# One mixture-of-experts tail: PSUM banks of its own for the fourth expert's result, ScalarE as the reader of all results but the last, and 4096 instead of 3584 columns of late weights in flight

## The chip, the cores and the metric

The kernel runs on one core of one Trainium2 chip. The metric is the device time of one execution in microseconds. The core has a matrix engine (TensorE, PE in the profile, with its weight loads shown apart as PEld), VectorE (DVE), ScalarE (ACT), GpSimd (POOL) and SyncE (SP), which issues most DMAs. Each engine does its own instructions strictly in the order written and waits for others through semaphores. TensorE writes to PSUM, eight banks of 2 KB for each of 128 partitions; VectorE and ScalarE read it from there. TensorE's clock is granted at 2.4 GHz (shown as 1.00) or 1.2 GHz (0.50).

## The reference

Attention with a soft cap, then a mixture of eight experts in which each token goes to one expert and each expert keeps at most 80 tokens:

```
scores = cap * tanh((q @ k.T) / sqrt(64) / cap);  attn = softmax(scores) @ v      # 8 x 12 heads, 448 x 64
x = attn as 3584 tokens x 768
logits = x @ w_gate                                # 768 x 8
expert = argmax(logits); gate = softmax(logits) at expert
for each expert with tokens: keep the 80 of largest gate
    out[kept] = gate[kept] * (relu(x[kept] @ w1[e]) @ w2[e])    # 768 x 1024, 1024 x 768
out of all other tokens = 0
```

## The kernel before

Attention is done for 48 pairs of heads in turn, TensorE and ScalarE being busy together. The gating logic (which tokens, in which order of gate) runs beside it on VectorE, GpSimd and ScalarE. After the last pair the tail begins: six experts that can have tokens, numbered 0 to 5 in the code (first to sixth in the text). The tokens of experts 0 to 3 are chosen from the first five batches and then corrected; those of experts 4 and 5 are known only after all rankings, so that their tokens are gathered (`xgv`, GpSimd, line 730) and transposed on VectorE (`lay`, line 1439, tile `xt`) in the middle of the tail.

The list `jobs` (line 743) fixes TensorE's order: first product of expert 0, then for each expert the first product of the next and the second of this one, as a0 a1 b0 a2 b1 a3 b2 b3 a4 a5 b4 b5. A first product has six chunks (`chunk`, line 782, tile `hp`, 32 matmuls of 80 columns each), a second product eight (`tokens`, line 792, tile `yt`, 18 matmuls of 192 or 384 columns). Between the chunks stand small products of the ranking: `pd` (line 433) counts, from 0/1 strips `gb` that VectorE makes (line 421), how many tokens come before each.

A first product goes to one of two pairs of banks (`pss`, tag `sc`) that are used in turn; `relu` (line 810, ScalarE) reads it. A second product goes to the two banks `yt0` and `yt1` of the pool `pf`, which all experts but the last share (line 1483), so that each must wait until the result before it has been read; the last uses two banks of the pool `ps1`. In a result, 80 tokens lie on partitions 0 to 79; the last quarter of the 768 columns lies on partitions 96 to 127 of both banks, in three pieces.

`weighed` (line 850) reads a result, weighs it by the gate `gt` and scatters it to HBM: VectorE copies the three pieces into the last quarter of the output tile `ywv` (line 855), ScalarE weighs the other three quarters while reading them (lines 856 and 857), VectorE weighs the last quarter in place (line 858), and GpSimd issues the scatter (line 859). There is one buffer of `ywv`. A result is read two chunks into the second product or the first product that follows it (`turns`, line 1489): the program's order on VectorE, ScalarE and GpSimd is that in which `background` (line 1283) and these calls emit their instructions.

The weights come in 84 loads of 128 rows, 1024 columns for a first product's chunk and 768 for a second's, in the order of `jobs`, through a ring of 22 buffers. `more` (line 753) adds to each load a wait for an earlier one, so that the loads from that one on have at most `FLIGHT` columns together: 5120 for the first 40 loads (`FULL`), 3584 after.

Of the kernel before, what the change touches and what calls it, by code (L numbers as in the profile page):

```python
# [7 lines left out]
F32 = mybir.dt.float32  # L8
# [3 lines left out]
AF = mybir.ActivationFunctionType  # L12
ALU = mybir.AluOpType
# [19 lines left out]
MV = 80  # L33
NV = 6
NPRE = 4
# [17 lines left out]
ODD = 'q0 q1 y b u a02 b q2 q3 x b a12 l n b'  # L53
NEXT = 'q0 q1 y b u a02 b q2 q3 x a12 l n b'
LAST = 'y q0 a00 a01 a10 a11 b a02 a12 u l n b m'
FLIGHT = (5120, 3584)
FULL = 40
PLACES = 4
GROUP = 835
# [63 lines left out]
def attn_moe(ctx, tc, q2, k, v, cap, wg, w1, w2, capacity, ct, out):  # L123
    nc = tc.nc
# [59 lines left out]
    si0 = consts.tile([SL, NPRE], I32, name="si0")  # L184
    sg0 = consts.tile([SL, NPRE], I32, name="sg0")
    gt0 = consts.tile([SL, NPRE], F32, name="gt0")
# [566 lines left out]
    def more(n):  # L753

        while len(wts) < min(n, len(jobs)):
            k_, v, kk = jobs[len(wts)]
            if v not in regs:
                src = ev0_i if v < NPRE else ev_i
                regs[v] = nc.values_load(src[0:1, v:v + 1], engines=[mybir.EngineType.SP], min_val=0, max_val=E - 1)
            wts.extend(wload(wring, regs[v], f"{v}", [kk if k_ == "a" else KD + kk], issued))  # L760
            i = len(issued) - 1
            room = FLIGHT[i >= FULL]
            while i >= 0 and room >= cols[i]:
                room -= cols[i]
                i -= 1
            if i >= 0:
                tc.add_manual_dep(issued[-1].ins, issued[i].ins.name, flight, reason="flight")
# [14 lines left out]
    def chunk(ps, x, w, kk, last, n, m=SL):  # L782

        per = n // 256
        ps = ps if isinstance(ps, list) else [ps[:, 0], ps[:, 1]]
        for j in range(n // 128):
            for h in range(2):
                nc.tensor.matmul(ps[j // per][64 * h:64 * h + 64, j % per * m:(j % per + 1) * m],  # L788
                                 w[:, 128 * j + 64 * h:128 * j + 64 * h + 64], x[:, kk, 0:m],
                                 start=(kk == 0 and j % per == 0), stop=(kk == last and j % per == per - 1))  # L790

    def tokens(ps, x, w, kk, last):


        q = DM // 4
        for r in range(2):
            for g in range(3):
                m = min(32, MV - 32 * g)
                y = slice(0, 2 * q) if r == 0 else slice(2 * q, 3 * q)
                nc.tensor.matmul(ps[r][32 * g:32 * g + m, 0:(2 - r) * q], x[:, kk, 32 * g:32 * g + m], w[:, y], start=kk == 0, stop=kk == last)  # L800
            for g in range(2 * r, 2 + r):
                m = min(32, MV - 32 * g)
                nc.tensor.matmul(ps[r][96:96 + m, g % 2 * q:g % 2 * q + q], x[:, kk, 32 * g:32 * g + m], w[:, 3 * q:4 * q],  # L803
                                 start=kk == 0 and g != 1, stop=kk == last and g > 0)
# [5 lines left out]
    def relu(fp, hp, tag, m=SL):  # L810
        th = fp.tile([128, KF, m], F32, name=f"th{tag}", tag="th")
        nc.scalar.activation(th.rearrange("p (a b) c -> p a (b c)", a=2), hp[:, :, 0:4 * m], AF.Relu)
        return th
# [33 lines left out]
                                     in_=ys.rearrange("p a b -> p (a b)"), in_offset=None,  # L847
                                     bounds_check=T - 1, oob_is_err=False)

    def weighed(fp, yt, gt, si, tag):  # L850
        q = DM // 4
        ys = fp.tile([MV, 4, q], F32, name=f"yw{tag}", tag="ys", bufs=1)
        for g in range(3):
            m = min(32, MV - 32 * g)
            nc.vector.tensor_copy(ys[32 * g:32 * g + m, 3], yt[g // 2][96:96 + m, g % 2 * q:g % 2 * q + q])
        nc.scalar.activation(ys[:, 0:2].rearrange("p a b -> p (a b)"), yt[0][0:MV, 0:2 * q], AF.Copy, scale=gt)  # L856
        nc.scalar.activation(ys[:, 2], yt[1][0:MV, 0:q], AF.Copy, scale=gt)  # L857
        nc.vector.tensor_scalar(ys[:, 3], ys[:, 3], gt, None, op0=ALU.mult)
        nc.gpsimd.indirect_dma_start(out=out, out_offset=bass.IndirectOffsetOnAxis(ap=si, axis=0),  # L859
                                     in_=ys.rearrange("p a b -> p (a b)"), in_offset=None,  # L860
                                     bounds_check=T - 1, oob_is_err=False)
# [170 lines left out]
    pss = at.enter_context(tc.tile_pool(name="pss", bufs=2, space=PSUM, side="right"))  # L1032
# [371 lines left out]
    fp = ft.enter_context(tc.tile_pool(name="fp", bufs=2, reuse_waits="tile"))  # L1404
# [6 lines left out]
    xv, fin = {}, {}  # L1411
# [47 lines left out]
    yt = {}  # L1459

    def out_(v):
        early_ = v < NPRE
        if v >= NV - 2:
            nc.gpsimd.drain()
        weighed(fp, yt[v], (gt0[:, v:v + 1] if early_ else fin["gt", v])[0:MV], (si0 if early_ else fin["si"])[0:MV, v:v + 1], f"v{v}")
    more(ahead(st["begun"]))
    turns = []
    for i, (k_, vi, kk) in list(enumerate(jobs))[st["begun"]:]:
        more(ahead(i))
        soon = jobs[min(i + 3, len(jobs) - 1)]  # L1470
        if soon[0] == "a" and soon[2] == 0 and soon[1] < NPRE - 1:
            st["there"](soon[1])
        if k_ == "a":
            if kk == 0:
                st["there"](vi)
                hp[vi] = pss.tile([128, 2, 512], F32, name=f"hp{vi}", tag="sc")
            chunk(hp[vi], xv[vi] if vi >= NPRE else xt0[vi], wts[i], kk, KD - 1, F, MV)
            if kk == KD - 1:
                ht[vi] = relu(fp, hp[vi], f"v{vi}", MV)
        else:  # L1480
            if kk == 0:
                if vi < NV - 1:
                    yt[vi] = [pf.tile([128, 512], F32, name=f"yt{vi}{i}", tag=f"yt{i}") for i in range(2)]
                else:
                    yt[vi] = [ps1.tile([128, 512], F32, name=f"yt{vi}{i}", tag="misc", bufs=2) for i in range(2)]
            tokens(yt[vi], ht[vi], wts[i], kk, KF - 1)
            if kk == KF - 1:
                turns.append(vi)
        if turns and (kk == 2 or i == len(jobs) - 1):
            out_(turns.pop())  # L1490
        background(4000, (1340, 1010)[k_ == "b"], TAIL)
# [52 lines left out]
```

## Time and profile before

| what | value |
|---|---|
| median of three runs (lowest to highest) | 486.61 us (485.44 to 486.83) |
| the profiled execution | 487.65 us, span 485.9 us |
| TensorE busy | 461.6 us, 95% of the span |
| ScalarE, GpSimd, VectorE busy | 340.1, 278.6, 278.0 us |
| granted clock of TensorE, mean | 0.986 |
| HBM traffic over the span | 202 GB/s |

The span is the time from the first to the last instruction of the profiled execution; the execution's time has 1.8 us more around it. Times in rows are microseconds from the span's start. A busy TensorE says little about where time is lost, since its matmuls are pipelined; what counts is where the rows of the tail show it idle or at the lower clock, and which engine ended the idle time.

### The profile page before, as it was taken

What the parts mean: (1) busy time and instruction counts of PE and PEld (TensorE: products, weight loads), DVE (VectorE), ACT (ScalarE), POOL (GpSimd) and SP (SyncE); (2) the same over time, 40 slices, a digit from 0 to 9 for tenths busy, and PEclk for the clock granted to TensorE, in tenths of its full rate; (3) what the DMA queues carried; (4) which work ended last, traced back from release to release, by engine and by line L of the source; (5) the groups of instructions that cost most, each with busy time, mean ns of one, the idle gap of its engine ahead of it and who ended that gap; (6) DMA issues with size and microseconds to landing.
All of it is one profiled execution on the core that took longest, in us unless ns stands there. A gap on an engine that the chain in (4) does not pass through costs nothing.

```text
span 485.9 us, 14488 instructions
## 1 busy us (share of the span) xinstructions
PE 461.6 (95%) x5864; PEld 197.2 (41%) x5864; DVE 278.0 (57%) x796; ACT 340.1 (70%) x360; POOL 278.6 (57%) x296
## 2 busy tenths in 40 slices
PE   6899999999999999999999999999999999969892
PEld 1222232223333223323233333324336887947882
DVE  1045446755664777579658957895668644633011
ACT  4999979988988998798888878886973444400010
POOL 1577686667667665776667585586496168060000
PEclk9899999999999999999999999999999999988998
DMA  5557478757836876764568377468269999999971
GB/s 150 149 163 206 110 182 240 213 139 189 228 94 168 234 189 172 185 185 133 138 169 225 100 195 209 111 190 240 71 161 387 386 349 336 336 327 306 293 267 32
DMA packets 68204, 99.09 MB, mean 204 GB/s; under 512 B 19328, under 2 KB 53152, under 8 KB 68128
## 3 DMA queue, kind: packets, MB, share of 16 engines
q1 hardware_dynamic: 63360, 83.82, 57.3%
q0 software_dynamic: 4640, 14.26, 11.3%
q8 instruction: 48, 0.79, 0.7%
q14 instruction: 28, 0.23, 0.2%
q10 hardware_dynamic: 128, 0.00, 0.0%
HBM read 74.54 MB, written 23.51 MB: 202 GB/s over the span
## 4 chain that ended last, share of the span: by engine, by line
PE 87%; DVE 4%; issue 4%; ACT 2%; DMA 2%; POOL 0%; SPq 0%; POOLq 0%; DVEq 0%; ACTq 0%
PE sc L1087 24%; PE av L1111 22%; PE hp L788 9%; PE yt L800 6%; PE sp L1159 4%; PE sc L1094 4%; PE yt L803 3%; PE sp L1160 3%; PE av L1140 3%; PE lgp L1203 3%; PE pd L433 2%; PE av L1130 2%; DMA xge<-xs,gi 1%; DVE prlh L569 1%; ACT e L1095 1%
## 5 line engine op out<-in xcount | busy, mean ns | idle before, releaser
L1095 ACT ACTIVATE e<-sc,scl 128x896 f32<-128x896 f32 x168 | 161.7, 1007 | 49.4 <-PE sc L1087 47.0
L1100 ACT ACTIVATE e<-e,capt 128x1792 f32<-128x1792 f32 x96 | 153.7, 1602 | 0.0
L1149 POOL TENSOR_TENSOR t<-e 128x448 f32<-128x448 f32 x96 | 108.9, 1157 | 75.1 <-ACT e L1100 75.1
L1087 PE MATMUL sc<-qt,kt 64*64 64x448 f32 x1152 | 135.3, 566 | 6.4 <-DMA qt<-in_q_dram 4.5
L1152 POOL TENSOR_TENSOR t<-t,e 128x448 f32<-128x448 f32 x96 | 108.7, 1153 | 48.9 <-ACT e L1100 38.7
L1111 PE MATMUL av<-e,vr 128*32 128x448 f32 x1152 | 132.0, 545 | 1.4 <-DVE x L1175 1.4
L1087 PEld LDWEIGHTS sc<-qt,kt 64*64 64x64 f32 x1152 | 35.8, 134 | 88.0 <-ACT e L1095 40.0
L1111 PEld LDWEIGHTS av<-e,vr 128*32 128x32 f32 x1152 | 32.7, 109 | 79.0 <-issue 62.9
L800 PE MATMUL yt<-w,thv 128*32 128x192 f32 (+3 forms) x576 | 51.4, 424 | 5.5 <-ACT ywv L856 4.8
L803 PE MATMUL yt<-w,thv 128*32 128x192 f32 (+1 forms) x288 | 51.5, 339 | 0.0
L1122 DVE TENSOR_SCALAR_CACHE_REDUCE sw<-e 64x896 f32<-64x896 f32 x32 | 34.6, 1080 | 25.8 <-ACT e L1100 25.3
L1163 DVE STREAM_TRANSPOSE st<-sp 128x448 f32<-128x448 f32 x24 | 15.6, 649 | 55.3 <-PE sp L1160 55.3
L788 PE MATMUL hp<-xt,w 128*64 128x80 f32 x1152 | 43.2, 234 | 2.2 <-issue 1.7
L788 PEld LDWEIGHTS hp<-xt,w 128*64 128x64 f32 x1152 | 40.9, 137 | 5.9 <-issue 5.4
L1175 DVE TENSOR_TENSOR x<-av,r 128x448 f32<-128x448 f32 x48 | 28.0, 619 | 24.3 <-PE av L1140 20.6
L424 ACT ACTIVATE gz<-gb 112x896 bf16<-112x896 bf16 (+12 forms) x22 | 18.5, 842 | 23.8 <-DVE gb L421 23.7
L859 POOL DMA_INDIRECT out_dram<-ywv,si x6 | 5.7, 944 | 47.6 <-ACT ywv L857 42.4
L803 PEld LDWEIGHTS yt<-w,thv 128*32 128x32 f32 (+1 forms) x288 | 30.6, 109 | 5.5
L426 DVE TENSOR_SCALAR_CACHE_REDUCE gb<-krow,kc 112x896 bf16<-112x896 f32 (+8 forms) x37 | 31.8, 884 | 0.0
L1189 POOL DMA_DIRECT2D xs<-xb x36 | 22.8, 642 | 10.6 <-DVE hs L277 10.6
L800 PEld LDWEIGHTS yt<-w,thv 128*32 128x32 f32 (+1 forms) x576 | 23.6, 109 | 11.0 <-ACT ywv L856 5.2
L1183 DVE STREAM_TRANSPOSE xb<-x 128x448 f32<-128x448 f32 x48 | 27.9, 619 | 0.1
(228 smaller groups left out, 436.6 us busy)
## 6 DMA issues: line engine op xcount, KB each, us to landing
w<-in_w_dram SPq DMA_DIRECT2D x36, 512.0 KB, 5.7
w<-in_w_dram SPq DMA_DIRECT2D x48, 384.0 KB, 5.5
kt<-in_k_dram SPq DMA_DIRECT2D x96, 112.0 KB, 2.8
qt<-in_q_dram SPq DMA_DIRECT2D x96, 112.0 KB, 2.8
xs<-xb POOLq DMA_DIRECT2D x28, 336.0 KB, 4.8
vr<-in_v_dram SPq DMA_DIRECT2D x40, 192.0 KB, 3.1
out_dram<-zero SPq DMA_DIRECT2D x4, 1536.0 KB, 6.7
out_dram<-zero SPq DMA_DIRECT2D x4, 1152.0 KB, 5.0
```

Source lines behind the costliest of these rows:

```text
L426: nc.vector.tensor_scalar(g, krow[:, x:y], kp, 0.0, op0=ALU.is_ge, op1=ALU.add, accum_out=a)
L788: nc.tensor.matmul(ps[j // per][64 * h:64 * h + 64, j % per * m:(j % per + 1) * m], w[:, 128 * j + 64 * h:128 * j + 64 * h + 64], x[:, kk, ...
L800: nc.tensor.matmul(ps[r][32 * g:32 * g + m, 0:(2 - r) * q], x[:, kk, 32 * g:32 * g + m], w[:, y], start=kk == 0, stop=kk == last)
L803: nc.tensor.matmul(ps[r][96:96 + m, g % 2 * q:g % 2 * q + q], x[:, kk, 32 * g:32 * g + m], w[:, 3 * q:4 * q], start=kk == 0 and g != 1, st ...
L1087: nc.tensor.matmul(ps[KR * i:KR * i + KR, h, :S], s["k"][w, x:x + KR], s["q"][w], start=True, stop=True)
L1095: nc.scalar.activation(s["e"][:, 2 * c:2 * c + 2], ps[:, :, :S], AF.Tanh, scale=scl)
L1100: nc.scalar.activation(x, x, AF.Exp, scale=capt)
L1111: nc.tensor.matmul(st["av", u, f][32 * g:32 * g + 32, :S], st[p]["v"][:, g % 2, c, 32 * f:32 * f + 32], st[p]["e"][:, 2 * c + g % 2], star ...
L1122: nc.vector.tensor_scalar(o[w], x[KR * (1 - a):KR * (1 - a) + KR, 2 * NK:2 * NK + 2], 1.0, 0.0, op0=ALU.mult, op1=ALU.add, accum_out=dump[w])
L1149: nc.gpsimd.tensor_tensor(t1[:, h], e[:, h], e[:, 2 + h], op=ALU.add)
L1152: nc.gpsimd.tensor_tensor(s["es"][:, h], s["es"][:, h], e[:, 4 + h], op=ALU.add)
L1175: nc.vector.tensor_tensor(x, st["av", u, f][:, :S], st["r", u], op=ALU.mult)
```

## The change

The fourth expert's result (`yt3`) goes to a pair of banks of the pool `pss`, as a first product does, and no longer to `yt0` and `yt1`. All results but the last are read by ScalarE alone: two weighing activations as before, three copies of the pieces, and one activation that weighs the last quarter in place. For the last result VectorE weighs the pieces as it reads them, by gates that it has copied to partitions 96 and up beforehand (`gw`), and ScalarE reads the second bank first. From load 40 on 4096 columns of weights may be in flight.

```
--- before.py
+++ after.py
@@ -53,7 +53,7 @@
 ODD = 'q0 q1 y b u a02 b q2 q3 x b a12 l n b'
 NEXT = 'q0 q1 y b u a02 b q2 q3 x a12 l n b'
 LAST = 'y q0 a00 a01 a10 a11 b a02 a12 u l n b m'
-FLIGHT = (5120, 3584)
+FLIGHT = (5120, 4096)
 FULL = 40
 PLACES = 4
 GROUP = 835
@@ -847,15 +847,24 @@
                                      in_=ys.rearrange("p a b -> p (a b)"), in_offset=None,
                                      bounds_check=T - 1, oob_is_err=False)
 
-    def weighed(fp, yt, gt, si, tag):
+    def weighed(fp, yt, gt, si, tag, gw=None):
         q = DM // 4
         ys = fp.tile([MV, 4, q], F32, name=f"yw{tag}", tag="ys", bufs=1)
-        for g in range(3):
-            m = min(32, MV - 32 * g)
-            nc.vector.tensor_copy(ys[32 * g:32 * g + m, 3], yt[g // 2][96:96 + m, g % 2 * q:g % 2 * q + q])
-        nc.scalar.activation(ys[:, 0:2].rearrange("p a b -> p (a b)"), yt[0][0:MV, 0:2 * q], AF.Copy, scale=gt)
-        nc.scalar.activation(ys[:, 2], yt[1][0:MV, 0:q], AF.Copy, scale=gt)
-        nc.vector.tensor_scalar(ys[:, 3], ys[:, 3], gt, None, op0=ALU.mult)
+        if gw is None:
+            nc.scalar.activation(ys[:, 0:2].rearrange("p a b -> p (a b)"), yt[0][0:MV, 0:2 * q], AF.Copy, scale=gt)
+            nc.scalar.activation(ys[:, 2], yt[1][0:MV, 0:q], AF.Copy, scale=gt)
+            for g in range(3):
+                m = min(32, MV - 32 * g)
+                nc.scalar.copy(ys[32 * g:32 * g + m, 3], yt[g // 2][96:96 + m, g % 2 * q:g % 2 * q + q])
+            nc.scalar.activation(ys[:, 3], ys[:, 3], AF.Copy, scale=gt)
+        else:
+            for g in range(3):
+                m = min(32, MV - 32 * g)
+                nc.vector.tensor_scalar(ys[32 * g:32 * g + m, 3], yt[g // 2][96:96 + m, g % 2 * q:g % 2 * q + q], gw[96:96 + m, g:g + 1], None, op0=ALU.mult)
+                if g == 0:
+                    nc.scalar.activation(ys[:, 2], yt[1][0:MV, 0:q], AF.Copy, scale=gt)
+                elif g == 1:
+                    nc.scalar.activation(ys[:, 0:2].rearrange("p a b -> p (a b)"), yt[0][0:MV, 0:2 * q], AF.Copy, scale=gt)
         nc.gpsimd.indirect_dma_start(out=out, out_offset=bass.IndirectOffsetOnAxis(ap=si, axis=0),
                                      in_=ys.rearrange("p a b -> p (a b)"), in_offset=None,
                                      bounds_check=T - 1, oob_is_err=False)
@@ -1462,7 +1471,7 @@
         early_ = v < NPRE
         if v >= NV - 2:
             nc.gpsimd.drain()
-        weighed(fp, yt[v], (gt0[:, v:v + 1] if early_ else fin["gt", v])[0:MV], (si0 if early_ else fin["si"])[0:MV, v:v + 1], f"v{v}")
+        weighed(fp, yt[v], (gt0[:, v:v + 1] if early_ else fin["gt", v])[0:MV], (si0 if early_ else fin["si"])[0:MV, v:v + 1], f"v{v}", fin["gw"] if v == NV - 1 else None)
     more(ahead(st["begun"]))
     turns = []
     for i, (k_, vi, kk) in list(enumerate(jobs))[st["begun"]:]:
@@ -1479,11 +1488,19 @@
                 ht[vi] = relu(fp, hp[vi], f"v{vi}", MV)
         else:
             if kk == 0:
-                if vi < NV - 1:
+                if vi == NPRE - 1:
+                    y = pss.tile([128, 2, 512], F32, name=f"yt{vi}", tag="sc")
+                    yt[vi] = [y[:, 0], y[:, 1]]
+                elif vi < NV - 1:
                     yt[vi] = [pf.tile([128, 512], F32, name=f"yt{vi}{i}", tag=f"yt{i}") for i in range(2)]
                 else:
                     yt[vi] = [ps1.tile([128, 512], F32, name=f"yt{vi}{i}", tag="misc", bufs=2) for i in range(2)]
             tokens(yt[vi], ht[vi], wts[i], kk, KF - 1)
+            if vi == NV - 1 and kk == 2:
+                gw = fin["gw"] = fp.tile([128, 3], F32, name="gw", tag="gw", bufs=1)
+                for g in range(3):
+                    m = min(32, MV - 32 * g)
+                    nc.vector.tensor_copy(gw[96:96 + m, g:g + 1], fin["gt", vi][32 * g:32 * g + m])
             if kk == KF - 1:
                 turns.append(vi)
         if turns and (kk == 2 or i == len(jobs) - 1):
```

On VectorE, at the place where the tokens of the fifth and sixth expert (tiles `xt`, from the gathered `xgv`) are transposed, stands before:

```order
L724 TENSOR_SCALAR sg<-sa 96x6
L1439 STREAM_TRANSPOSE xt_5679<-xgv_0_5584 128x6x32
L1439 STREAM_TRANSPOSE xt_5679<-xgv_1_5586 128x6x32
L1439 STREAM_TRANSPOSE xt_5679<-xgv_2_5588 128x6x32
L855 COPY ywv_5705<-yt_5493 32x192 x2
L855 COPY ywv_5705<-yt_5494 16x192
L858 TENSOR_SCALAR ywv_5705<-ywv_5705,gt_110 80x192
L1439 STREAM_TRANSPOSE xt_5789<-xgv_0_5590 128x6x32
```

and now (line numbers are those of the changed kernel):

```order
L724 TENSOR_SCALAR sg<-sa 96x6
L1448 STREAM_TRANSPOSE xt_5678<-xgv_0_5584 128x6x32
L1448 STREAM_TRANSPOSE xt_5678<-xgv_1_5586 128x6x32
L1448 STREAM_TRANSPOSE xt_5678<-xgv_2_5588 128x6x32
L1448 STREAM_TRANSPOSE xt_5788<-xgv_0_5590 128x6x32
```

The read of the third expert's result (`yt_5493`, `yt_5494`) has left VectorE, where it stood behind the fifth expert's three transposes.

On ScalarE, at the first expert's result (`yt_4762`, `yt_4763`), between the ranking's sums (`gz`) and the relu of the third expert (`thv_5113`), stands before:

```order
L424 ACTIVATE gz_7_4932,acc_94<-gb_7_4930 112x896
L424 ACTIVATE gz_7_4960,acc_94<-gb_7_4930 112x768
L856 ACTIVATE ywv_5016<-yt_4762,gt_110 80x384
L857 ACTIVATE ywv_5016<-yt_4763,gt_110 80x192
L812 ACTIVATE thv_5113<-hp_4936 128x640
```

and now:

```order
L424 ACTIVATE gz_7_4960,acc_94<-gb_7_4930 112x768
L854 ACTIVATE ywv_5016<-yt_4762,gt_110 80x384
L855 ACTIVATE ywv_5016<-yt_4763,gt_110 80x192
L858 COPY ywv_5016<-yt_4762 32x192 x2
L858 COPY ywv_5016<-yt_4763 16x192
L859 ACTIVATE ywv_5016<-ywv_5016,gt_110 80x192
L812 ACTIVATE thv_5113<-hp_4936 128x640
```

Three copies and one scaling have come to ScalarE; the order on GpSimd and TensorE is the same as before.

## Rows read from the trace of the kernel before

**Rows 1.** the page, part 4: the chain that ended last, shares by engine

```profile
PE 87%; DVE 4%; issue 4%; ACT 2%; DMA 2%; POOL 0%; SPq 0%; POOLq 0%; DVEq 0%; ACTq 0%
```

**Rows 2.** timeline of TensorE: start us, duration us, line, tiles, form, [idle before <-releaser]

```profile
428.72 0.52 PE L800 MATMUL yt<-w,thv 128*16 128x384 f32 x3
...
429.69 0.52 PE L800 MATMUL yt<-w,thv 128*16 128x384 f32 x3
...
435.64 0.85 PE L800 MATMUL yt<-w,thv 128*32 128x384 f32 x3 [4.76 <-ACT ywv L856]
...
446.27 11.33 PE L788 MATMUL hp<-xt,w 128*64 128x80 f32 x316
...
476.05 0.49 PE L800 MATMUL yt<-w,thv 128*32 128x384 f32 x3
```

**Rows 3.** timelines of VectorE and ScalarE at the hole

```profile
433.73 0.38 DVE L1439 STREAM_TRANSPOSE xt<-xgv 128x192 f32<-128x192 f32 x1 [1.48 <-DMA xgv<-xs,gi]
434.12 1.12 DVE L855 COPY ywv<-yt 32x192 f32<-32x192 f32 x3
...
435.01 0.58 ACT L856 ACTIVATE ywv<-yt,gt 80x384 f32<-80x384 f32 x1 [10.26 <-issue]
```

**Rows 4.** table by stretch: length, busy PE, PEld, DVE, ACT, POOL, clock, DMA share, GB/s

```profile
364.00:388.00 24.00, 24.00 (x510) 17.91 (x502) 17.16 (x60) 8.46 (x21) 9.75 (x10) 1.00 1.02 387
...
447.00:468.00 21.00, 19.63 (x491) 18.05 (x491) 0.61 (x2) 2.29 (x4) 0.94 (x1) 1.00 0.90 291
...
435.60:446.30 10.70, 10.66 (x146) 7.06 (x146) 3.35 (x18) 0.30 (x1) 1.09 (x2) 0.74 0.95 322
...
455.00:460.00 5.00, 3.63 (x105) 3.49 (x103) 0.00 (x0) 0.00 (x0) 0.00 (x0) 1.00 0.97 343
```

**Rows 5.** weight loads (line 776), all from 408 on, then the last alone

```profile
L776 SPq DMA_DIRECT2D w<-in_w_dram x41: 332/333/1287, 408.3 to 467.4; - x41
...
L776 SPq DMA_DIRECT2D w<-in_w_dram x1: 332/332/332, 467.4 to 467.4; - x1
...
DMA to landing us min/median/max: 4.9/4.9/4.9
```

**Rows 6.** timelines of ScalarE, GpSimd, VectorE and weight loads of TensorE, first result

```profile
398.70 0.58 ACT L856 ACTIVATE ywv<-yt,gt 80x384 f32<-80x384 f32 x1
399.18 0.41 ACT L857 ACTIVATE ywv<-yt,gt 80x192 f32<-80x192 f32 x1
...
400.24 0.96 POOL L859 DMA_INDIRECT out_dram<-ywv,si  x1 [1.49 <-ACT ywv L857]
...
406.22 0.20 POOL L494 TENSOR_TENSOR fpos<-fcmp 128x8 f32<-128x8 f32 x1
...
406.46 0.22 DVE L374 TENSOR_TENSOR fcmp<-fpos,ctt 128x64 f32<-128x64 f32 x1 [4.75 <-POOL fpos L494]
...
410.87 0.89 PEld L433 LDWEIGHTS <-gb 112*128 112x128 bf16 x33 [0.32 <-DVE gb L421]
```

**Rows 7.** timelines of VectorE, ScalarE and GpSimd, last result

```profile
477.05 1.12 DVE L855 COPY ywv<-yt 32x192 f32<-32x192 f32 x3 [6.29 <-PE yt L803]
...
477.94 0.58 ACT L856 ACTIVATE ywv<-yt,gtv 80x384 f32<-80x384 f32 x1 [6.88 <-DVE ywv L855]
...
479.31 0.91 POOL L859 DMA_INDIRECT out_dram<-ywv,si  x1 [6.84 <-ACT ywv L857]
```

**Rows 8.** GpSimd's gathers, then landing of late gathers, early gathers, second scatter

```profile
428.29 0.95 POOL L730 DMA_INDIRECT xgv<-xs,gi  x1 [0.31 <-issue]
...
434.54 0.93 POOL L1432 DMA_INDIRECT gtv<-gd,sg  x1 [0.30 <-issue]
...
DMA to landing us min/median/max: 5.4/5.4/5.4
...
DMA to landing us min/median/max: 5.7/6.0/7.9
...
DMA to landing us min/median/max: 6.0/6.0/6.0
```

## The prediction, written before the changed kernel was run

> **What bounds the kernel now.** Read first the chain of waits on the page: it is 87% TensorE, so a change counts where it lets TensorE start earlier or run at a higher clock [rows 1]. The change touches only the experts' stage at the end, so the second view is TensorE's timeline there. Its one long hole lies between the third expert's last chunk of second weights (first matmul at 429.69) and the fourth expert's first (435.64), and its row names the ScalarE read of the third result (L856) as what ended it [rows 2]. The third view is the timeline of VectorE and ScalarE around that hole: the third result was complete near 430.7, but VectorE first had to do the three transposes of the fifth expert's tokens, the last at 433.73; its copies of the result came behind them at 434.12, and ScalarE, which waits until VectorE has left the bank, read at 435.01 [rows 3]. So a strict order on VectorE, behind a gather, holds TensorE. The fourth view is the table by stretch: after the hole the clock was granted at 0.74 on average over the fourth expert's second product (part of it at 1.2 GHz), against 1.00 in the stretches before and after [rows 4]. Last the weights: the final one is issued at 467.4 and lands 4.9 later, at 472.3 [rows 5]; its first matmul is at 476.05 [rows 2]. So weights have 3.8 us in hand at the end, and no more.
>
> **The change part by part.**
>
> *Banks of its own for the fourth result (gain).* TensorE no longer waits for the third result to be read: the two banks taken were left by the third expert's first product, which ScalarE had read long before. A chunk's pitch at full clock is 429.69 - 428.72 = 0.97, so the fourth product can start at 429.69 + 0.97 = 430.66 instead of 435.64: 4.98 less [rows 2]. Its eight chunks lasted 446.27 - 435.64 = 10.63 [rows 2]; at 0.97 each they last 7.76. The clock fell after the hole and only there, so this 2.87 goes too. Together 7.85. What could be late next is the fifth expert's tokens. Their third gather is issued at 428.29 and transposed from 433.73 to 434.1 [rows 3, 8]; the fifth expert now starts at 430.66 + 7.76 + 1.25 (the delay below) = 439.7, so about 4.4 are left even if this chain moves by the same 1.25.
>
> *The new wait.* The fourth result now lies in the pair of buffers that the sixth expert's first product takes next, so that product waits for ScalarE's read of the fourth result; and this read writes the one output buffer, so it waits until the third result's scatter has landed. Queued behind it on ScalarE is the relu of the fifth expert, wanted only after the sixth's first product. The scatter stands behind the eight gathers on GpSimd, the last issued at 434.54 for 0.93; moved by 1.25 it goes at about 437.0. With the 6.0 of an earlier scatter it lands at 443.0 [rows 8], and the last PSUM read is about 1.7 later, at 444.7. The sixth expert's product starts six chunks after the fifth's: 316 matmuls of this kind took 11.33, so 192 take 6.88 [rows 2], and it starts at 446.6. Cost: nothing, 1.9 in hand; from a landing time of 7.9 on every microsecond costs one.
>
> *Results read by ScalarE alone (loss at the first result).* For five results it takes two activations, three copies and one scaling where it took two activations. From start to start 399.18 - 398.70 = 0.48 for the wide one; the 192-column one lasts 0.41 and overlaps the next by 0.10 as the pair does, so 0.31 for it and each copy, 0.2 for the wait on its own writes before the scaling (an estimate: in the tail ScalarE starts some 0.15 after VectorE's second copy [rows 7]), 0.41 for the scaling: 0.48 + 4 x 0.31 + 0.2 + 0.41 = 2.33 against 0.89 now [rows 6]. It starts some 0.2 sooner, as no VectorE copy stands before it, and so is done 1.25 later. For the first result this matters: GpSimd holds its scatter at 400.24 until ScalarE is done, and behind it stand two gathers and the folds that end with fpos at 406.22, with hardly a gap; VectorE waits for fpos until 406.46, makes the comparison strips, and TensorE waits for those at 410.87 [rows 6]. TensorE is already waiting there, so all of 1.25 is added. Bounds: 0, if ScalarE's pieces overlap so far that GpSimd's present idle time of 1.49 gets no longer, and 1.6, if no piece overlaps the next. I take 1.25. For the results two to five nothing stands behind ScalarE that TensorE wants within 2 us: no cost, and at the third result the cover is 4 us of gathers.
>
> The Trainium skill, page "ScalarE: Activation LUTs", section "What ACT_TABLE_LOAD costs", gives an activation without a pointer operand 0.186 us + 0.833 ns per column and one pointer operand 0.093 more. By it a 192-column copy is 0.346 and this term an estimated 1.08; its 0.439 for the scaled form stands against 0.41 in the trace, so the measured rows are used.
>
> *Tail of the last result (small gain).* Before: three VectorE copies from 477.05, ScalarE from 477.94, the scatter issued at 479.31, 2.26 after TensorE [rows 7]. Now VectorE weighs while it reads, 0.36 each, and ScalarE begins on the other bank at once: bank one is free after two reads at 0.76, ScalarE's wide read 0.92 to 1.50, scatter 0.48 behind: 1.98. Gain 0.28; bounds 0 and 0.6.
>
> *4096 columns in flight.* Late weights of 768 columns go five at a time instead of four, those of 1024 four instead of three. TensorE now needs the last weight at 476.05 - (7.85 - 1.25) = 469.45, and it lands at 472.3: the stream must gain 2.8 in the 59 us from 408.3 [rows 5], or 5%. No run shows 4096. Bounds: the late stage moved 291 to 322 GB/s with three or four in flight, the earlier one 387 with five or six [rows 4]. A value between by the columns in flight is about 340, an estimate; even a third of the way, 320, is 10%. So I take it that weights are in time. The term is 0; its other end is the 2.8 lost in full, and nothing can be gained beyond it.
>
> **Sum.** -4.98 - 2.87 + 1.25 - 0.28 = -6.88. The profiled execution took 487.65 (span 485.9 and 1.8 around it), 1.0 above the median of the three runs, 486.61; the terms are stalls and counts that do not scale with it, so 480.8 for a profiled execution and 479.7 for the median.
>
> **The rivals.**
>
> 1. The weights bind: with a stream no faster, the last chunk starts at 472.3 and TensorE ends 1.0 later, at 473.3 instead of 477.05; with the tail -4.0, or 482.6. For it: a DMA share of 0.90 and 0.95 in the late stretches. Against it: the share was 1.02 with 387 GB/s [rows 4].
> 2. The new wait of some 1.5 at the comparison strips (410.9) drops the clock as the old hole did: another 2.87, -4.0, or 482.6. Against it: between 455 and 460 TensorE was busy for 3.63 of 5 us and the clock stayed at 1.00 [rows 4].
> 3. The change only moves the wait: the sixth expert's product waits for ScalarE behind the scatter. With a landing of 9.4 the time is 481.2, and with 14.8 nothing is left of the gain. GpSimd's transfers in the rows take 7.9 at most [rows 8].
> 4. Slower than before: more weights in flight starve the fifth expert's gathers, which are on another queue. The gather takes L from its issue at 429.5; TensorE waits for L - 9.6, and from a wait of 4.8 on the clock halves as it did before (2.87). It is slower by more than can be told from no change from L = 15.1 on; at 16 it is +2.4, 489.0. Rows: 5.4 in the late stage, 6.0 median and 7.9 at most in the stage with 5120 in flight [rows 8], so half of what it needs.
>
> To rival 4 belongs a rule of the Trainium skill that speaks against the change, page "DMA: Bandwidth & Descriptors", section "Issuing engines are not separate DMA queues": what SP and GpSimd issue runs on the same 16 DMA engines and interleaves. By that rule the gathers pay for every weight added; the trace agrees in sign, 5.4 against up to 7.9, and its size stays inside the 4.4 that are free.
>
> **How the numbers follow.** The forecast, 479.7, has 0.70; its own range by the bounds of the terms is 478.1 (no loss at the first result, tail 0.6) to 481.2 (loss 1.6, tail 0, and 0.9 for weights that are in time only in part). Rival 1 has 0.13, rival 2 0.06, rival 3 0.04, rival 4 0.04; 0.03 are left for a gain beyond 478. The range to 483.0 takes in rivals 1 and 2; down to 478.0. What a measurement of this kernel can tell from no change is about 0.3%, 1.5 us, so the forecast and rivals 1 and 2 and most of 3 are faster: 0.92; no change, the middle of rivals 3 and 4: 0.04; slower: 0.04.
>
> **What would show it.** Right: no idle time before the fourth expert's second product, which lasts 7.8 at a clock of 1.00; TensorE waiting about 1.5 for the strips near 411 to 412, with GpSimd's first scatter near 401.5; the weights' last landing before 469; scatter about 2.0 after TensorE's end. Wrong: idle time at the second product of experts five and six that ends on a weight (rival 1), a second stretch of half clock (2), a wait of the sixth expert's first product on ScalarE (3), of the fifth's on VectorE's transposes (4).

## The result, and the profile after

Median of six runs: 480.22 us (479.12 to 482.57), against 486.58 for the kernel before in as many; ratio 0.988, 95% interval 0.986 to 0.991. The forecast was 479.7, and its mechanism is what the trace shows, but for one term. Yet in a later round, on a chip where the kernel before takes 500.0 us, the same change brings nothing (ratio 1.000, 0.997 to 1.002); on each of the four chips of the experiments the kernel before took 498 to 500, and the larger part of the study is about why.

The chain that ended last has more of TensorE than before [rows 1], since the hole is gone:

```profile
PE 92%; DVE 3%; ACT 1%; issue 1%; DMA 1%; SPq 0%; POOL 0%; POOLq 0%; DVEq 0%
```

The table of waits of TensorE in the stage (engine, line, what it waited for: us, times, longest), after and then before. The 4.76 us for ScalarE at the fourth expert's second product [rows 2] is not in it any more; what is left, 1.4 us in the sixth expert's first product, stood there before as well:

```profile
engine line waited for: us in total, times, longest us
PE hp L788 <- issue: 1.4, 1, 1.4
```

```profile
PE yt L800 <- ACT ywv L856: 4.8, 1, 4.8
PE hp L788 <- issue: 1.4, 1, 1.4
```

The table by stretch, after, in the columns of [rows 4]: the third expert's second product up to the start of the fourth's, then the fourth's. The same two of the kernel before are below it. Between them lie the two gains of the prediction: 13.75 to 9.01 for the hole, 10.63 to 8.32 for the clock, which is 1.00 now where it was 0.74. (With no hole between them the matmuls of the two products overlap, so that the boundary at 429.44 is read to about 0.1; the sum of the two is not touched by it.)

```profile
420.43:429.44 9.01, 9.01 (x186) 7.56 (x188) 1.42 (x9) 1.17 (x4) 3.92 (x5) 1.00 0.97 354
...
429.44:437.76 8.32, 8.32 (x151) 6.98 (x142) 2.54 (x9) 2.28 (x6) 4.72 (x6) 1.00 1.01 376
```

```profile
421.89:435.64 13.75, 8.99 (x185) 7.21 (x185) 3.94 (x16) 1.79 (x6) 7.56 (x8) 0.95 0.95 338
...
435.64:446.27 10.63, 10.63 (x144) 7.03 (x145) 3.32 (x18) 0.26 (x1) 1.09 (x2) 0.74 0.95 321
```

The timelines after that answer to [rows 3]: VectorE does the fifth expert's last transpose at 433.80, which is 13.4 after the start of the third expert's second product where it was 11.8 before, but the result's read no longer stands behind it; ScalarE read the third result at 429.53, the moment it was complete. The third row is ScalarE's read of the fourth result, held until the third's scatter has landed:

```profile
433.80 0.38 DVE L1448 STREAM_TRANSPOSE xt<-xgv 128x192 f32<-128x192 f32 x1 [0.78 <-DMA xgv<-xs,gi]
...
429.53 0.58 ACT L854 ACTIVATE ywv<-yt,gt 80x384 f32<-80x384 f32 x1 [6.24 <-PE yt L803]
...
440.36 0.58 ACT L854 ACTIVATE ywv<-yt,gt 80x384 f32<-80x384 f32 x1 [8.48 <-DMA out_dram<-ywv,si]
```

The profiled execution took 479.12 us (span 477.3), 8.5 less than that of before. Of this 1.9 is not the change's: it is there before the first of the changed instructions (VectorE's copy `nesn`, at 396.85 before, stands at 394.96). 1.5 of it stands already behind a stretch near the start in which the kernel before had a half clock in its profiled execution and the changed one had not (VectorE reads its first sum `sw` at 24.80 before and 23.34 after); the other 0.4 comes between 360 and 370, where the kernel before waits 0.46 for a transpose of gathered rows and the changed one does not. The rest, 6.6, is set against the prediction below. The rows for 14 to 18 us, before and then after:

```profile
14.00:18.00 4.00, 3.66 (x24) 1.08 (x24) 0.00 (x0) 3.46 (x5) 3.43 (x4) 0.57 0.57 163
```

```profile
14.00:18.00 4.00, 3.16 (x32) 0.72 (x24) 0.00 (x0) 4.00 (x5) 3.15 (x3) 1.00 0.54 161
```

### The profile page after: what moved, and what is told of

It is laid out like the page before. It is cut to its first block, busy times and chain, and to the rows that moved or that the text cites. A ratio compares the mean times of both kernels' runs of the same rounds, so it can differ in the third digit from the quotient of the medians.

```text
span 477.3 us, 14483 instructions
## 1 busy us (share of the span) xinstructions
PE 457.4 (96%) x5864; PEld 196.6 (41%) x5864; DVE 271.8 (57%) x778; ACT 346.7 (73%) x380; POOL 278.6 (58%) x296
## 4 chain that ended last, share of the span: by engine, by line
PE 92%; DVE 3%; ACT 1%; issue 1%; DMA 1%; SPq 0%; POOL 0%; POOLq 0%; DVEq 0%
PE sc L1096 25%; PE av L1120 24%; PE hp L788 9%; PE yt L800 7%; PE sp L1168 4%; PE sp L1169 4%; PE sc L1103 3%; PE yt L803 3%; PE av L1149 3%; PE lgp L1212 3%; PE pd L433 2%; PE av L1139 2%; DVE prlh L569 1%; PE lt L1229 1%; PE psk L404 1%
## 5 line engine op out<-in xcount | busy, mean ns | idle before, releaser
L1096 PE MATMUL sc<-qt,kt 64*64 64x448 f32 x1152 | 133.3, 558 | 7.3 <-DMA qt<-in_q_dram 4.7
L800 PE MATMUL yt<-w,thv 128*32 128x384 f32 (+3 forms) x576 | 49.2, 407 | 0.7 <-issue 0.7
L803 PE MATMUL yt<-w,thv 128*32 128x192 f32 (+1 forms) x288 | 49.1, 327 | 0.0
```

The costliest lines, as they stand in the source:

```text
L1096: nc.tensor.matmul(ps[KR * i:KR * i + KR, h, :S], s["k"][w, x:x + KR], s["q"][w], start=True, stop=True)
```

## Experiments

### One part at a time

E1 has the banks alone, E2 the columns alone, E3 the reading by ScalarE and the new tail on the old banks with 3584 columns, E4 the whole change but with 3584 columns. The edits, to the kernel before (E1, E2) and to the changed one (E3, E4):

```
E1: -                if vi < NV - 1:
    +                if vi == NPRE - 1:
    +                    y = pss.tile([128, 2, 512], F32, name=f"yt{vi}", tag="sc")
    +                    yt[vi] = [y[:, 0], y[:, 1]]
    +                elif vi < NV - 1:
E2: -FLIGHT = (5120, 3584)
    +FLIGHT = (5120, 4096)
E3: E1 undone, and as E4
E4: -FLIGHT = (5120, 4096)
    +FLIGHT = (5120, 3584)
```

> The kernel before with one edit: the fourth expert's result in banks of its own; VectorE reads as before and late weights stay at 3584 columns. Theory M (the hole and its half clock are the gain, the weights then bind): no idle time before the fourth product, no second stretch at 1.2 GHz, but TensorE waits about 4 us in all for weights in the products of the fifth and sixth expert, since the last weight lands as before near 472: 482.8, that is 3.8 less than before. Theory S (ScalarE's earlier read is the gain, not the banks): 486.6, no change. Theory F (the weights in flight are the gain): 486.6. If weights do not bind at all: 478.8.

> The kernel before with one edit: 4096 columns of late weights in flight. Theory M: the hole stays, and grows by the 1 to 1.5 us by which the fifth expert's third gather lands later (5.4 before, 6.9 in the changed kernel): 487 to 488, not faster. Theory F (the weights are the gain): about 482. Theory S: 486.6.

> The kernel before with one edit: all results but the last read by ScalarE alone, the last weighed by VectorE while it reads; banks and 3584 columns as before. Theory M: TensorE still waits for the third result to be read, but only for ScalarE's 2 us behind the product (about 2.4 instead of 5.0). If that shorter wait leaves the clock at 2.4 GHz, the gain is held by the weights at about 4: 482.6; if the clock falls, 484. Theory S: as the changed kernel but for weights, 482.6. So the wait and the clock in the trace decide, not the time. Theory F: 486.6.

> The changed kernel with 3584 columns of late weights instead of 4096: both other parts of the change stay. Theory M with rival 1's price: the weights bind, TensorE waits 2 to 3 us for them in the last products, last landing near 472 on the scale of the kernel before: 482.6, about 2.4 over the changed kernel. If the weights were never late: 480.2, the same as the changed kernel, or below it if more weights in flight slow TensorE.

Measured, as ratios to the kernel before, which took 498.1 us on this chip and not 486.6: E1 0.997 (0.995 to 1.000), E2 1.002 (1.000 to 1.004), E3 1.001 (0.998 to 1.004), E4 0.998 (0.996 to 1.001). None of the expected steps is there, so the parts could not be told apart here. The trace of E2 shows why there is little to gain. The first row is from the third expert's second product to the fourth's start, the second the fourth's; then the wait between them:

```profile
430.75:450.98 20.23, 15.77 (x187) 8.42 (x185) 3.99 (x17) 1.80 (x6) 7.55 (x8) 0.83 0.96 347
450.98:458.92 7.94, 7.94 (x145) 6.22 (x145) 2.97 (x18) 0.25 (x1) 1.08 (x2) 1.00 1.00 362
```

```profile
450.98 0.52 PE L800 MATMUL yt<-w,thv 128*32 128x384 f32 x3 [0.93 <-ACT ywv L856]
```

The hole that ScalarE ends is 0.93 and not 4.76, although E2 reads the result behind the transposes as the kernel before does. The third expert's second product itself is stretched by pauses of TensorE for which the trace names nobody ("issue"). While it is stretched, the gathers land and the transposes are done, so that VectorE is free when the result is complete. In none of these four traces does TensorE wait for weights.

### The change itself there, and wider or narrower

E5 is the changed kernel itself, E6 has banks and 4096 columns with the old reading (E1 and E2 together), E8 is E1 again, and E7 is the changed kernel with

```
-FLIGHT = (5120, 4096)
+FLIGHT = (5120, 5120)
```

> The changed kernel itself, once more. Theory M (the hole before the fourth expert's second product is what the change takes out): where the kernel before has that hole, as in its first profile (486.6 us), the time is 480.2, ratio 0.987. On a chip like that of the first four experiments (before 498.1), where TensorE stalls inside the third expert's second product and the read of the third result is done meanwhile, there is only about 1 us of hole to take: ratio 0.996 to 1.000. Rival T (4096 columns in flight and ScalarE's reading bring something of their own): ratio 0.990 or less there too.

> The kernel before, with the fourth result's banks of its own and 4096 columns in flight, but the results read by VectorE and ScalarE as before. Theory M: the reading by ScalarE alone is not needed, since with banks of its own nobody on TensorE waits for the third result. It loses the tail's 0.14 and keeps the first result's 0.24: the time of the changed kernel within 0.5 us, ratio to it 1.000. Rival R (the late read of the third result on VectorE, behind the fifth expert's transposes, holds up the fifth or sixth expert): 1.5 us or more above the changed kernel, with a wait of TensorE on VectorE or ScalarE in the fifth or sixth expert's products.

> The changed kernel with 5120 columns of late weights in flight instead of 4096. Theory M: weights have 3.8 us in hand with 4096 already, so nothing is gained: the time of the changed kernel within 0.5 us, and the last weight lands 2 to 4 us earlier. Rival C (the weights' traffic slows TensorE: in the changed kernel's profile its chunks of the fourth expert's second product took 1.04 instead of 0.97 us): the time rises by 0.5 to 1.5 us over the changed kernel, and that product lasts over 8.3 us. Rival I (weights that come sooner help): 0.5 or more below it.

> Banks of its own alone (3584 columns in flight, results read as before), a second time, since in the first run of this kernel TensorE's stalls hid the hole. Theory M: where before takes 486.6, the hole's 4.98 and the half clock's 2.87 go, but the weights then bind, as their last lands about 2.8 us too late: 482.8, ratio 0.992. Rival S (the banks alone bring nothing, because the third result's read still comes behind the transposes and something else waits for it): 486.6, ratio 1.000. Rival G (they bring all of it, weights do not bind): 480.2, ratio 0.987. Where before takes about 498: ratio 0.997 as in the first run by all three.

They ran on another chip again, where the kernel before took 500.0. E5 1.000 (0.997 to 1.002), E6 1.001 (0.998 to 1.004), E7 1.000 (0.998 to 1.003), E8 0.996 (0.994 to 0.999). That is what theory M has for such a chip (hardly a hole, hardly a gain), and rival T's 0.990 is outside E5's interval. That 4096 columns slow TensorE is not borne out: E7 with 5120 is no slower than E5. One wait for weights, 0.9 us, stands in E6's trace, and none in the others. E8 is a little faster than the rest, as E1 was; its interval overlaps theirs a little, and what it is due to stays open.

The stretches of E5, then its waits in the first, then the first and the last of GpSimd's eight late gathers. The two stretches together are 28.18, with the banks of the change, against 28.17 in E2 without them. Single traces of this kind differ, though: E3, on the old banks too, has 27.64, and E1, E4, E6, E7 and E8 on the new ones have 26.19 to 27.58. So the 1 to 2 us that the medians of E1 and E8 are below the kernel before can be neither seen nor ruled out in single traces, but nothing near the 7 of the first runs is there:

```profile
431.76:451.19 19.43, 14.73 (x187) 8.46 (x188) 3.72 (x16) 1.17 (x5) 7.56 (x8) 0.86 0.97 350
451.19:459.94 8.75, 8.75 (x150) 7.30 (x142) 2.36 (x16) 2.38 (x6) 1.08 (x2) 0.92 0.97 335
```

```profile
PE yt L800 <- issue: 3.5, 5, 1.1
PE yt L803 <- issue: 1.0, 2, 0.6
```

```profile
436.16 0.97 POOL L730 DMA_INDIRECT xgv<-xs,gi  x1 [7.28 <-DVE sg L724]
...
444.92 0.92 POOL L1441 DMA_INDIRECT gtv<-gd,sg  x1 [0.30 <-issue]
```

TensorE falls behind its pitch 2 us after the first of these gathers starts (438.2) and is back at it 2 us after the last is over (447.6). Two more groups of pauses, 371 to 381 and 408 to 413, stand beside other groups of gathers. But gathers alone do not make pauses: beside the group from 351.55 to 356.3, during attention, TensorE is busy all through, with fewer instructions and less DMA traffic than in the experts' stage:

```profile
351.00:358.00 7.00, 7.00 (x76) 2.41 (x68) 3.20 (x12) 4.14 (x6) 5.91 (x7) 1.00 0.57 117
```

### The gathers made plain copies

P1 is the changed kernel, P2 the kernel before, P3 is E4 and P4 is E6, each with the 18 gathers of token rows replaced by copies of 128 fixed rows of the same size, so that the choice of the tokens is left out:

```
-        nc.gpsimd.indirect_dma_start(out=xg, out_offset=None, in_=xs[0:n].rearrange("t i p c -> (t i) (p c)"),
-                                     in_offset=bass.IndirectOffsetOnAxis(ap=gi, axis=0))
+        gk = fp.tile([128, 1], I32, name=f"gk{tag}", tag="gk", bufs=3)
+        nc.gpsimd.tensor_copy(gk, gi)
+        nc.gpsimd.dma_start(xg, xs[n - 32:n].rearrange("t i p c -> (t i) (p c)"))
```

> The changed kernel with the 18 gathers of token rows (12 xge, 6 xgv) made plain copies: GpSimd copies the index column (so that it waits for it as before) and then issues a plain DMA of 128 fixed rows of the same 192 columns. It leaves out the choice of the tokens, so the outputs are of other tokens. In the changed kernel on the chip of the second four experiments TensorE's stalls stood only while GpSimd issued indirect DMAs: 372.6 to 382 (gathers 366.9 to 379.9), 409 to 413.6 (405.5 to 412.4), 438.5 to 447.5 (436.2 to 445.8). Theory G (the indirect gathers stall TensorE's instruction supply there): with plain copies the stalls go, the third expert's second product lasts about 9.5 instead of 17, and the time falls by 8 to 14 us. Theory W (weights' traffic starves it): the same bytes are moved, the stalls stay, the time changes by less than 3. Theory P (any DMA that GpSimd issues does it): the stalls stay, though shorter as the issues take less time. On a chip without the stalls: within 2 us of 480.

P1 took 480.15 us in one run, on a chip where the kernel before took 498.4, as where the pauses were traced. Of theory G this shows that the pauses need the indirect gathers, and not that instructions come late. The fall is 18 and not 8 to 14 us. The same weights are moved, so W falls, and GpSimd still issues each copy (0.55 us instead of 0.95), so P falls too. An indirect DMA as such is not enough either: P1 still issues the two gathers of gates (`gtv`) in that form, and beside them TensorE is busy all through. Three stretches with gathers in them, first of E5, then of P1. In the second column TensorE is busy for 13.54 of 18, 3.62 of 6 and 7.54 of 12 us in E5, 11.3 us of idle time, and all through in P1. Part of what else went is the clock, 0.86 and 0.92 in the two stretches of E5 above and 1.00 here. The two gathers of gates in P1 stand below its stretches:

```profile
364.00:382.00 18.00, 13.54 (x221) 8.74 (x219) 8.60 (x25) 3.44 (x11) 10.32 (x11) 0.97 0.82 290
408.00:414.00 6.00, 3.62 (x85) 3.19 (x87) 0.23 (x1) 0.54 (x2) 4.29 (x9) 1.00 1.02 405
436.00:448.00 12.00, 7.54 (x72) 3.19 (x67) 1.82 (x6) 0.00 (x0) 7.56 (x8) 0.91 0.94 335
```

```profile
364.00:382.00 18.00, 18.00 (x394) 14.00 (x388) 10.20 (x41) 4.79 (x13) 6.47 (x13) 1.00 1.03 393
408.00:414.00 6.00, 6.00 (x132) 4.37 (x126) 4.98 (x19) 5.22 (x10) 3.10 (x10) 1.00 0.96 325
424.00:436.00 12.00, 12.00 (x220) 9.97 (x216) 3.23 (x14) 2.84 (x9) 7.14 (x16) 1.00 1.00 370
```

```profile
429.88 0.98 POOL L1442 DMA_INDIRECT gtv<-gd,sg  x1 [0.30 <-issue]
431.17 0.95 POOL L1442 DMA_INDIRECT gtv<-gd,sg  x1 [0.30 <-issue]
```

With the pauses gone, the change and its parts can be compared on such chips:

> The kernel before with the same 18 plain copies for the gathers of token rows (fixed rows, so other tokens), to compare with the changed kernel in that form, 480.15 us in one run. Theory M (the change is worth the hole and the half clock behind it, wherever TensorE isn't stalled by the gathers anyway): in that one run the fifth expert's third transpose stood at 432.79, so that VectorE's copies come at 433.2, ScalarE's read at 434.1 and the fourth expert's second product at about 434.7 instead of 430.58: a hole of 4, with up to 2.9 for the clock; 485 to 487 us. Rival N (without the stalls the change has no worth of its own): 480 to 481.

> The changed kernel with plain copies and 3584 columns of late weights in flight. It leaves out the choice of the tokens. Theory M (the first rival of the prediction with its 2.8 us: at 3584 the weights bind): 482 to 483.5 us, with idle time of TensorE in the sixth expert's second product. Rival F (weights don't bind at 3584 either): 480 to 481, last weight issued some 9 us later than 459.1. Rival T (fewer columns in flight let TensorE run its chunks at 0.97 instead of 1.04): 479 to 480.

> Banks of its own and 4096 columns, the results read by VectorE and ScalarE as in the kernel before, with plain copies. It leaves out the choice of the tokens. Theory M (the reading by ScalarE alone isn't what brings the time; it loses 0.24 at the first result and gains 0.14 at the last): 480.1, within 0.5 of the changed kernel in that form. Rival R (the read of the third result behind the transposes holds up the sixth expert or the tail): 481.5 or more. Rival C (the prediction's term of 1.25 at the first result was right): 479.2.

All three ran on one chip, where the kernel before took 499.9. P2 484.88 us (ratio 0.972, 0.969 to 0.974), P3 484.40 (0.969, 0.966 to 0.971), P4 480.61 (0.962, 0.959 to 0.965).

P2 differs from the kernel before by the copies alone, so these are worth 15.0 us there. P2 to P4 is 4.3 us with intervals well apart: without the pauses the hole is back, and banks with 4096 columns take it out. P2's row of the fourth expert's start, and its two stretches:

```profile
433.92 0.85 PE L801 MATMUL yt<-w,thv 128*32 128x384 f32 x3 [4.27 <-ACT ywv L857]
```

```profile
420.66:433.92 13.26, 8.99 (x186) 7.13 (x185) 3.99 (x17) 1.79 (x6) 6.03 (x14) 0.98 0.97 336
433.92:443.25 9.33, 9.33 (x144) 6.56 (x144) 2.96 (x18) 0.26 (x1) 1.10 (x2) 0.85 0.88 296
```

P3 has the new banks and is hardly better than P2, 484.40 where 482 to 483.5 was expected. The hole is gone all the same: its two stretches, the first two rows below, are 17.33 together as in the changed kernel, which also says that 4096 columns do not slow TensorE there. What the banks gain is lost again in the last two second products, 19.82 in P3 (third row) against 15.80 in P2 (below it): here the weights bind, and the waits of TensorE name them (the row of the largest below the table):

```profile
421.22:429.99 8.77, 8.77 (x186) 7.31 (x189) 1.41 (x9) 1.17 (x4) 4.63 (x13) 1.00 0.92 324
429.99:438.55 8.56, 8.45 (x152) 7.26 (x142) 4.43 (x23) 2.39 (x6) 2.52 (x4) 1.00 0.99 340
452.63:472.45 19.82, 17.21 (x290) 10.59 (x288) 0.19 (x1) 2.98 (x7) 0.91 (x1) 1.00 0.80 278
```

```profile
457.87:473.67 15.80, 15.80 (x290) 13.16 (x288) 1.62 (x5) 1.59 (x3) 0.91 (x1) 1.00 0.76 258
```

```profile
PE yt L801 <- DMA w<-in_w_dram: 2.6, 5, 1.3
```

```profile
468.76 0.52 PE L801 MATMUL yt<-w,thv 128*32 128x384 f32 x3 [1.31 <-DMA w<-in_w_dram]
```

P4, which reads as the kernel before did, is 0.5 from P1's one run, on another chip (0.962 of the kernel before there, P1 0.963): the reading by ScalarE alone isn't needed for the gain. So P3 and P4, which differ in it too, are 3.8 us apart by the 4096 columns. Without these the banks bring 0.5, with intervals that overlap: the two go together.

The two stretches in one table (us):

| | third expert's second product, to the start of the fourth's | fourth's | sum |
|---|---|---|---|
| first runs: before, after | 13.75, 9.01 | 10.63, 8.32 | 24.38, 17.33 |
| other chips: old banks (E2), changed kernel (E5) | 20.23, 19.43 | 7.94, 8.75 | 28.17, 28.18 |
| plain copies: old banks (P2), changed kernel (P1) | 13.26, 8.95 | 9.33, 8.41 | 22.59, 17.36 |
| plain copies: new banks with 3584 columns (P3) | 8.77 | 8.56 | 17.33 |

The kernel before was not traced on the other chips; E2 and E3, which keep its banks, stand for it.

## Why the prediction was right, point by point

*The hole.* Predicted 4.98, measured 4.74 (13.75 - 9.01). The fourth expert starts with no idle time.

*The clock.* Predicted 2.87, measured 2.31. The clock is 1.00 throughout, as forecast. (Rival 4's "from a wait of 4.8 on" is no boundary: in P2 a hole of 4.27 was followed by a clock of 0.85.) The product lasts 8.32 instead of 7.76. Two places make up about that: the first row below, of TensorE's timeline, takes 0.81 where its like take 0.5, and there is a gap of 0.32 in its weight loads at the change to the next product (second row), which was inside the 10.63 before and which 8 x 0.97 leaves out:

```profile
433.43 0.81 PE L800 MATMUL yt<-w,thv 128*32 128x384 f32 x3
...
437.76 0.34 PEld L788 LDWEIGHTS hp<-xt,w 128*64 128x64 f32 x8 [0.32 <-issue]
```

*The loss at the first result: the step that failed.* Predicted 1.25, measured 0.43 in all up to the third expert's second product (421.89 to 420.43, less the 1.89). ScalarE's part was right: 2.33 predicted, 396.59 to 398.93 measured, 1.23 later against the rest of the program. Then the links behind it swallowed some. GpSimd's scatter, first row, came 0.86 later and not 1.25 (idle time before it 1.49 to 2.35 [rows 6]); `fpos` and VectorE 0.84. TensorE's strips lost 0.27, the second row against its like in [rows 6], 0.89 to 1.16. That is all that came through this chain. About as much, 0.26, was lost earlier, at the third expert's first product, where a pause for which the trace names nobody grew from 0.35 to 0.61 (the last two rows, before and after); 0.1 came back later:

```profile
399.21 0.96 POOL L868 DMA_INDIRECT out_dram<-ywv,si  x1 [2.35 <-ACT ywv L859]
...
409.20 1.16 PEld L433 LDWEIGHTS <-gb 112*128 112x128 bf16 x33 [0.32 <-issue]
```

```profile
400.29 2.02 PE L788 MATMUL hp<-xt,w 128*64 128x80 f32 x52 [0.35 <-issue]
```

```profile
398.66 2.02 PE L788 MATMUL hp<-xt,w 128*64 128x80 f32 x52 [0.61 <-issue]
```

"TensorE is already waiting there, so all of 1.25 is added" was the mistake. The gap of 0.32 read from row 410.87 was taken for a wait on VectorE, whose name the row gives; the same 0.32 stands there now with "issue", and at 437.76 above, where nobody is late. So it is what a change of product costs here, and the strips had half a microsecond in hand: in the kernel before VectorE's last strip was done at 411.09 and TensorE's weight loads of the strips at 411.76, after at 410.19 and 410.36. The lower bound of the term, 0, was nearer than its value.

*Tail.* Predicted gain 0.28, measured 0.14: from VectorE's first read to the scatter 2.12 (468.86 to 470.98) against 2.26 [rows 7]. Three weighing reads take 1.33 instead of 1.12:

```profile
468.86 1.33 DVE L863 TENSOR_SCALAR ywv<-yt,gw 32x192 f32<-32x192 f32 x3 [28.57 <-PE yt L803]
...
470.98 0.91 POOL L868 DMA_INDIRECT out_dram<-ywv,si  x1 [6.39 <-ACT ywv L867]
```

*Columns in flight.* The term of 0 held: the last weight was issued at 457.7, landed 6.3 later, and was used 3.8 after that. The late stream moved 369 GB/s against 291 to 322 [rows 4], above the 340 estimated. The term's other end, 2.8 if 3584 had stayed, measured 3.8 in P3 against P4, with plain copies: the first rival was real and was kept out by this edit alone. The rows after, of the late stretch (last column GB/s) and of the last weight load:

```profile
420.00:440.00 20.00, 20.00 (x408) 17.11 (x404) 5.83 (x31) 3.44 (x10) 8.64 (x10) 1.00 0.99 369
```

```profile
L776 SPq DMA_DIRECT2D w<-in_w_dram x1: 333/333/333, 457.7 to 457.7; - x1
...
DMA to landing us min/median/max: 6.3/6.3/6.3
```

*The other rivals.* No second stretch of half clock (2). The sixth expert's product started at 444.81 with no wait for ScalarE, whose last read of the fourth result was over by 442.2 (3): the scatter landed 6.0 after its issue, as assumed. The fifth expert's third gather landed after 7.0 us instead of 5.4 (4), far from the 15.1 that this rival needed; its transpose was over at 434.18, 3.6 before the fifth expert started. The landing times in us, least, median and most, of those four of the six gathers of line 730 for which the trace has one:

```profile
DMA to landing us min/median/max: 6.0/6.6/7.0
```

The Trainium skill's page "DMA: Bandwidth & Descriptors", section "Issuing engines are not separate DMA queues", has DMAs interleave on the same 16 DMA engines, whichever engine issued them. The sign, 1.6 us later with more weights in flight, agrees.

*The sum.* -4.74 - 2.31 + 0.43 - 0.14 = -6.76, and 0.32 more for the four products after the fourth's (31.01 to 31.33), 0.19 less behind the scatter: -6.63 against -6.88. The hole and the clock fell short by 0.8 and the loss by as much, so it is luck that the total is closer than its terms.

What the prediction didn't have is that the whole gain hangs on TensorE not being stalled while the gathers run. No row of the kernel before shows such a stall, and none of the rivals was that. That the first runs had none of it is luck too: on all four chips used afterwards the kernel before took 498 to 500.

## What to carry to other kernels

When a wait is removed, work out at once what is late next: here the banks were worth about 0.5 us without the columns (P3) and 4.3 with them (P4). A short gap in front of an instruction is a wait only if it is longer than the gap that stands before its like where nobody is late. And a hole on the bounding engine can be covered by a stall that other runs of the same program have and these haven't: time such a change on more than one chip, and compare stretches, not only totals.

## What the runs showed of the hardware

The same kernel took 486.6 us in the first runs and 498 to 500 us on the four chips of the experiments. On the two of these where kernels with the gathers were traced, TensorE paused in the experts' stage while GpSimd issued indirect gathers of token rows; on a third, with plain copies of the same size the kernel before took 484.9 instead of 499.9. The pauses come in steps of about 0.72 us, with a few instructions in between, as in these rows of E5:

```profile
444.04 0.32 PE L800 MATMUL yt<-w,thv 128*16 128x192 f32 x1 [0.24 <-issue]
444.77 0.32 PE L800 MATMUL yt<-w,thv 128*16 128x192 f32 x1 [0.41 <-issue]
...
445.50 0.32 PE L803 MATMUL yt<-w,thv 128*16 128x192 f32 x1 [0.39 <-issue]
```

On which chip the first runs were made is not known, so that the chip makes the difference is likely, but not shown. What it would be on the chip stays open, and so does whether it is the indirect form of these gathers or the scattered rows: P1 changes both at once.

In every kernel's page 48 packets and 0.79 MB stand for a queue of instructions, 16 KB a packet; by its size it is TensorE's, which has 11728 of the changed kernel's 14483. The Trainium skill's page "Runtime: NRT & Kernel Launch", section "Instruction fetch mechanics", has an engine fetch its instructions in blocks of 16 KiB through a DMA queue of its own, at a cost that is mostly hidden. The size agrees. Whether the pauses are late instructions is a guess, since the trace says only that TensorE waited for nothing that it shows. By the same numbers a packet is some 240 instructions, and between two of the pauses there are only a few, so a packet that is late as a whole would not explain the steps.

```profile
q8 instruction: 48, 0.79, 0.7%
```
